# Filter blocks and the shift convolution turned by transposing transfers, with channels on partitions

## The chip, the cores and the metric

The kernel runs on one core of a Trainium2 chip. The metric is the device time of one execution in microseconds (us). The time before is the median of three runs, 225.92 us (225.48 to 226.31).

A core has four computing engines that run beside each other: PE (matrix products; its weight loads are shown as PEld), DVE (elementwise work), ACT (activations, scaled copies), and POOL (small elementwise work). SP only issues transfers. Transfers run on 16 DMA engines. Each engine works through its own list in order and waits on semaphores.

## The reference

```
x = A_q                                   # 2048 x 640, bf16
g = sigmoid(sum(x * gate_w, -1))          # one gate per row

# a: shift convolution, product, long convolution along the sequence, output product
k_shift[s] = sum over t = 0..3 of k[s - t] * shift_k[:, t]
kv = k_shift * v
y  = causal convolution of kv with ssm_k along the sequence, per channel
a  = q * (y + kv * ssm_D)

# b: LayerNorm over channels, then an MLP that mixes the sequence
h = layernorm(x)
u = gelu(h^T w1 + b1)                     # 640 x 1536
b = (u w2 + b2)^T
out = g * a + (1 - g) * b
```

The filter `ssm_k` comes with channels in rows (640 x 2048); q, k and v come with the sequence in rows (2048 x 640).

## The kernel before

The long convolution is cut into P = 4 blocks of n = 512 positions (NB = 4 tiles of 128). Filter block i and input block j are transformed with sine and cosine tables of length 1024. There are four sets of 128 frequencies (fi = 0 and 1 the odd ones, 2 and 3 the even ones), with a cosine and a sine part each. Z for output block m is the sum over j of A_j times W_(m-j), and each Z is transformed back. The products A * W and their sums run on DVE (`pair`); forward and backward transforms run on PE.

The filter: `wnat_load` brings block i with channels on partitions. `w_time` (called for each block ahead of `w_freq`) turns it with 20 matmuls against an identity matrix, and ACT copies four 128x640 results to `wT`. `split` forms sums and differences of the block's halves (`ee`) on DVE. `transform` then makes 48 matmuls per block: two tiles of `ee` per result for even frequencies, four tiles of `wT` for odd ones, the latter with the negated tables `TN`. ssm_D is added to the filter's first position.

The input: `kv_load` brings, for each of the 16 tiles of 128 positions, k with its three predecessors (a row of `k4` holds four rows of k, so k is read four times over), and v. `kv_tile` multiplies `k4` on DVE by `shkb` (shift_k copied to all partitions by eight matmuls), and sums the four taps on PE by matmuls against the identity, or against the flip matrix for the two later tiles of a block, whose v is flipped by PE and ACT as well. ACT copies the sum to `kvb`, DVE multiplies it by v. `a_split` forms sums and differences (`es`), and `a_freq` makes 32 matmuls per block and eight copies on ACT to `A`.

The MLP: `h` has one tile per 128 rows of x; DVE makes the statistics, and POOL the root. The first MLP product takes w1 in six sets of two columns of 128 (`w1_load`), the second takes w2 (`mlp2`).

Nothing of the order is written by hand. All operations are given to a planner (`_Plan`), which books a cost and a latency for each, books a transfer at 0.30 MB per us plus 2 us, and ranks the operations by a priority (the argument `pr`) and by the length of the work that hangs on them. It then places each on its engine in time, which fixes the engine's order. Four results of two PSUM banks each (`_PS`) can be open at once. `_Tracker` places the waits. Every transfer but the later w1 sets and w2 (POOL) is issued from SP. Buffers have fixed places in SBUF; they hold k4 four deep, v five deep, `kvb` and `es` once.

Line numbers in the profile are those of helpers: L290 is every matmul, L676 every DVE tensor_tensor, L718 every ACT operation, L258 every transfer. So work is told apart by its tiles.

Of the kernel before, what the change touches and what calls it, by code (L numbers as in the profile page):

```python
# [17 lines left out]
class _Tracker:  # L18
# [227 lines left out]
    def dma(self, stream, out_ap, in_ap, semname, noncontig=False, accum=False):  # L246
# [5 lines left out]
        if accum:  # L252
            ins = engobj.dma_start(out_ap, in_ap, accum_op=ALU.add)
# [263 lines left out]
def _build(nc, A_q, A_k, A_v, A_shift_k, A_ssm_k, A_ssm_D, B_x, B_w1, B_b1, B_w2, B_b2, gate_w, out):  # L517
# [15 lines left out]
    with ExitStack() as es:  # L533
# [28 lines left out]
        buf("bf", [128, FT + NT], F32, 0, END)  # L562
        buf("brow", [FT + NT, 128], BF16, 0, 30)
# [14 lines left out]
        buf("ident", [128, 128], BF16, 0, END)  # L578
        buf("flip", [128, 128], BF16, 0, END)
        buf("flipn", [128, 128], BF16, 0, END)  # L580
        buf("Dv", [128, D], BF16, 0, 40)
        buf("TFc", [128, 1024], BF16, 0, 48)
        buf("TFs", [128, 1024], BF16, 0, 48)
        buf("TN", [128, 2, 256], BF16, 0, 48)
# [10 lines left out]
        for i in range(P):  # L595
            buf(f"wnat{i}", [128, DC, n], BF16, 0, 16 + 6 * i)
            buf(f"wT{i}", [128, NB, D], BF16, 5 + 5 * i, 24 + 7 * i)
        for i in range(2):
            buf(f"ee{i}", [128, NB, D], BF16, 8, (40, 46)[i])
        for i in range(P):  # L600
            buf(f"W{i}", [128, 9, D], BF16, 14 + 8 * i, END)
        buf("shk1", [1, D, KS], BF16, 0, 20)
        buf("ones", [1, 128], BF16, 0, 20)
        buf("shkb", [128, KS, D], BF16, 5, 84)
        KR = 4
        VR = 5
        for i in range(VR):
            buf(f"v_{i}", [128, D], BF16, 30 + 2 * i, 84)
        KVB = 1
        for i in range(KR):  # L610
            buf(f"k4_{i}", [128, KS, D], BF16, 30 + 2 * i, 84)
        buf("tT", [128, 8, D], BF16, 42, END)
        for i in range(KVB):
            buf(f"kvb{i}", [128, NB, D], BF16, 44, 90)
        for i in range(1):
            buf(f"es{i}", [128, NB, D], BF16, 48, 90)
# [57 lines left out]
        def tt(out_, in0, in1, op, pr, eng="DVE"):  # L674
            c = 0.07 + nel(out_) / 1920.0 if eng == "DVE" else 0.3 + nel(out_) / 500.0
# [46 lines left out]
        def dma(out_ap, in_ap, semname, pr, stream="SP", noncontig=False):  # L722
# [6 lines left out]
            def emit():  # L729
                T.dma(stream, out_ap, in_ap, semname, noncontig=noncontig)  # L730
# [3 lines left out]
        def pe(pslist, mms, pr, after=()):  # L734
# [4 lines left out]
            cost = sum(0.016 + m[2] * 0.000372 for m in mms)  # L739

            def emit():
                full = [(pp[p_.slot][:, c0:c0 + w_], lhsT, rhs, st, sp) for (p_, c0, w_, lhsT, rhs, st, sp) in mms]
                T.mm_part(full)
# [20 lines left out]
        memset(cst[:, 4:5], 2.0 / N2, 0)  # L764
        memset(cst[0:1, 4:5], 0.0, 0)
        memset(cst[:, 5:6], -float(n), 0)
        memset(cst[:, 6:7], -float(N2), 0)
        c_pi, c_hp, c_mh, c_w, c_w0, c_mn, c_mn2 = (cst[:, i:i + 1] for i in range(7))
# [12 lines left out]
        ts(b["ident"][:, :], b["id_i"][:, :], 0.0, None, ALU.is_equal, None, 0.2, eng="POOL")  # L781
# [33 lines left out]
        TN = b["TN"]  # L815
        for nb in range(2):
            c0 = nb * 512 + 256
            ts(TN[:, nb, 0:128], TFs[:, c0:c0 + 128], -1.0, None, ALU.mult, None, 0.5, eng="POOL")
            ts(TN[:, nb, 128:256], TFc[:, c0 + 128:c0 + 256], -1.0, None, ALU.mult, None, 0.5, eng="POOL")
        ts(b["par_i"][:, :], b["ncol_i"][:, 0:1], 1, None, ALU.bitwise_and, None, 0.6, eng="DVE")  # L820
        for nb in range(2):
            ts(TFs[:, nb * 512:nb * 512 + 1], b["par_i"][:, :], -2.0, 1.0, ALU.mult, ALU.add, 0.6, eng="DVE")
# [9 lines left out]

        def to(c, nb, fi):
            if nb < 2:
                return tf((TFc, TFs)[c], nb, fi)
            nb -= 2
            if c == fi:
                return TN[:, nb, fi * 128:fi * 128 + 128]
            return tf((TFs, TFc)[c], nb, fi)
# [66 lines left out]
        dma(b["Dv"][0:1, :], dram(A_ssm_D, 0, [[D, 1], [1, D]]), "Dv", 0.06)  # L906
# [8 lines left out]
        dma(b["brow"][0:FT, :], dram(B_b1, 0, [[128, FT], [1, 128]]), "b", 1.5)  # L915
        dma(b["brow"][FT:FT + NT, :], dram(B_b2, 0, [[128, NT], [1, 128]]), "b", 1.5)
        p_ = _PS()
        pe([p_], [(p_, 0, FT + NT, b["brow"][:, :], b["ident"][0:FT + NT, 0:FT + NT], True, True)], 2)
        act(b["bf"][:, :], (lambda p_: lambda: pp[p_.slot][:, 0:FT + NT])(p_), ACT.Copy, 2, ps=[p_])
        dma(b["shk1"][:, :, :], dram(A_shift_k, 0, [[D * KS, 1], [1, D * KS]]), "shk", 1.6)  # L920
        memset(b["ones"][:, :], 1.0, 2)
        for j in range(KS):
            p_ = _PS()
            pe([p_], halves(p_, [(b["ones"][:, :], b["shk1"][:, :, KS - 1 - j])]), 0.9)
            act(h2(b["shkb"][:, j, :]), two(p_), ACT.Copy, 0.9, ps=[p_])

        def w_time(i):
            wn = b[f"wnat{i}"]
            wT = b[f"wT{i}"]
            for k in range(NB):  # L930
                p_ = _PS()
# [302 lines left out]
```

## Time and profile before

| what | us |
|---|---|
| median of three runs | 225.92 |
| span of the profiled execution, first to last instruction | 222.4 |
| PE busy, 1481 matmuls | 202.8 |
| DVE busy, 253 instructions | 201.8 |
| ACT busy, 221 instructions | 139.9 |
| POOL busy | 41.5 |

The profile has no time of its own execution besides the span; the median lies 3.5 us above that. A group's line reads: engine, operation, tiles written <- read, shapes, count | total busy us, mean ns of one | idle time of the engine just before them, and what ended it. In the chain each line has a start, a length and what ran. In the slices a digit is the busy share in tenths of one fortieth of the span.

### The profile page before, as it was taken

The numbers are of one execution on the slowest core, as the hardware profiler recorded it, in microseconds if no ns is written. First come the engines' busy times: TensorE is split into PE (matmuls) and PEld (weight loads), VectorE is DVE, ScalarE is ACT, GpSimd is POOL, SyncE is SP. The second block draws the span as 40 slices with busy tenths as digits, with TensorE's granted clock in tenths as the row PEclk, the third lists the DMA queues.
The fourth block names the chain that finished last, engine by engine and source line by source line (L and its number), as shares of the span: only waits on it lengthen the run. The fifth ranks groups of instructions, "written<-read, shape, count | busy, mean of one in ns | idle before, by whom it ended". The sixth has DMA issues, their size and how long they took to land.

```text
span 222.4 us, 3751 instructions
## 1 busy us (share of the span) xinstructions
PE 202.8 (91%) x1481; PEld 141.1 (63%) x1481; DVE 201.8 (91%) x253; ACT 139.9 (63%) x221; POOL 41.5 (19%) x79
## 2 busy tenths in 40 slices
PE   0829799999998998999999999999999999999991
PEld 0725547567675774777777777667777777767651
DVE  3379999899988998999999999999999999999771
ACT  4899988997579869683746511799431845432251
POOL 8563330301131010015171010000101101110000
PEclk9988999999999999999999999999999999999997
DMA  6999996139915894899962114302065845286003
GB/s 180 359 325 349 235 298 244 43 109 304 347 41 146 297 391 160 287 295 294 288 181 58 36 16 140 119 3 59 0 202 169 244 116 180 83 253 200 0 3 118
DMA packets 22087, 39.88 MB, mean 179 GB/s; under 512 B 1715, under 2 KB 17205, under 8 KB 22069
## 3 DMA queue, kind: packets, MB, share of 16 engines
q1 hardware_dynamic: 18964, 28.10, 39.8%
q0 software_dynamic: 3104, 11.54, 17.9%
q8 instruction: 12, 0.20, 0.4%
q14 instruction: 7, 0.05, 0.1%
HBM read 36.35 MB, written 2.62 MB: 175 GB/s over the span
## 4 chain that ended last, share of the span: by engine, by line
PE 60%; DVE 22%; ACT 11%; DMA 5%; issue 1%; DVEq 0%; SPq 0%
PE pp L290 60%; DVE Z L676 10%; DVE tT L676 7%; DMA k<-in_A_k_dram 3%; ACT wT L718 2%; ACT W L718 2%; DMA wnat<-in_A_ssm_k_dram 2%; ACT L718 1%; DVE es L676 1%; DVE cg L676 1%; ACT kvb L718 1%; DVE kvb L676 1%; DVE k L676 1%; DVE xg L676 1%; ACT TFs L718 1%
## 5 line engine op out<-in xcount | busy, mean ns | idle before, releaser
L290 PE MATMUL pp<-h,w 128*128 128x320 bf16 x384 | 54.9, 299 | 0.0
L290 PE MATMUL pp<-gT,w 128*128 128x320 bf16 x384 | 53.1, 299 | 0.0
L676 DVE TENSOR_TENSOR tT<-A,W 128x640 bf16<-128x640 bf16 (+4 forms) x44 | 48.0, 1121 | 0.3
L676 DVE TENSOR_TENSOR Z<-Z,tT 128x2560 bf16<-128x2560 bf16 (+3 forms) x35 | 47.1, 1370 | 0.1
L290 PEld LDWEIGHTS pp<-gT,w 128*128 128x128 bf16 x384 | 37.5, 98 | 14.8 <-issue 0.3
L290 PEld LDWEIGHTS pp<-h,w 128*128 128x128 bf16 x384 | 37.5, 98 | 14.6
L258 POOL DMA_DIRECT2D w<-in_B_w_dram x18 | 17.3, 962 | 117.7 <-PE pp L290 117.1
L718 ACT ACTIVATE o<-pp,c,omg 128x640 bf16<-128x640 f32 x16 | 14.2, 884 | 31.4 <-PE pp L290 31.4
L676 DVE TENSOR_TENSOR k<-k,shkb 128x2560 bf16<-128x2560 bf16 x16 | 23.4, 1485 | 0.6 <-DMA k<-in_A_k_dram 0.5
L718 ACT ACTIVATE A<-pp 128x640 bf16<-128x640 f32 x32 | 20.0, 717 | 2.0 <-PE pp L290 2.0
L718 ACT ACTIVATE gT<-pp,bf 128x640 bf16<-128x640 f32 x12 | 9.5, 792 | 18.3 <-PE pp L290 18.2
L290 PE MATMUL pp<-Z,TI 128*128 128x320 bf16 x128 | 18.4, 299 | 1.1 <-ACT kvb L718 1.1
L718 ACT ACTIVATE W<-pp 128x640 bf16<-128x640 f32 x24 | 15.9, 707 | 3.9 <-PE pp L290 3.8
L290 PE MATMUL pp<-ident,wnat 128*128 128x128 bf16 x80 | 8.0, 274 | 10.1 <-DMA wnat<-in_A_ssm_k_dram 5.4
L290 PEld LDWEIGHTS pp<-Z,TI 128*128 128x128 bf16 x128 | 12.4, 98 | 6.4 <-ACT kvb L718 1.4
L718 ACT ACTIVATE kvb<-pp 128x640 bf16<-128x640 f32 x16 | 11.2, 701 | 5.8 <-PE pp L290 5.8
L290 PEld LDWEIGHTS pp<-ident,wnat 128*128 128x128 bf16 x80 | 6.6, 124 | 11.2 <-DMA wnat<-in_A_ssm_k_dram 5.8
L893 DVE BATCH_NORM_STATS2 stats<-xs 128x6 f32<-128x320 bf16 x32 | 13.3, 475 | 0.0
L718 ACT ACTIVATE xg<-xg 128x640 bf16<-128x640 bf16 x16 | 11.6, 734 | 1.7 <-DVE xg L676 1.7
L676 DVE TENSOR_TENSOR Z<-A,W 128x5120 bf16<-128x5120 bf16 x4 | 11.3, 2819 | 0.7 <-ACT A L718 0.7
L290 PE MATMUL pp<-wT,TFc 128*128 128x320 bf16 x48 | 10.1, 300 | 1.7 <-ACT W L718 1.7
L290 PE MATMUL pp<-es,AFs 128*128 128x320 bf16 x64 | 10.1, 300 | 0.8 <-ACT gT L718 0.8
(92 smaller groups left out, 279.2 us busy)
## 6 DMA issues: line engine op xcount, KB each, us to landing
k<-in_A_k_dram SPq DMA_DIRECT2D x15, 640.0 KB, 7.7
w<-in_B_w_dram POOLq DMA_DIRECT2D x8, 768.0 KB, 5.8
w<-in_B_w_dram POOLq DMA_DIRECT2D x10, 512.0 KB, 6.1
wnat<-in_A_ssm_k_dram SPq DMA_DIRECT2D x4, 640.0 KB, 6.5
v<-in_A_v_dram SPq DMA_DIRECT2D x16, 160.0 KB, 7.4
xg<-in_A_q_dram SPq DMA_DIRECT2D x8, 320.0 KB, 7.1
xe<-in_A_q_dram SPq DMA_DIRECT2D x8, 320.0 KB, 3.1
out_dram<-cg SPq DMA_DIRECT2D x8, 320.0 KB, 4.3
```

The source lines that it names most:

```text
L258: ins = engobj.dma_start(out_ap, in_ap)
L290: ins = self.nc.tensor.matmul(ps_ap, lhsT=lhsT, rhs=rhs, start=start, stop=stop)
L676: return vop(eng, c, lambda e: e.tensor_tensor(out_, in0, in1, op), [in0, in1], [out_], pr)
L718: return e.activation(out_, src, func, **kw)
L893: vop("DVE", 0.41, (lambda o_, i_: lambda e: e.bn_stats(o_, i_))(o_, i_), [i_], [o_], pr)
```

## The change

Channels lie on partitions for the filter and for the shift convolution. Transfers that transpose (`dma_start_transpose`, all issued from SP) take the place of turns on PE.

The filter: DVE folds a block while channels are on partitions: the later half plus and minus the earlier half read backwards, from position 256 outwards (`en`); position 0, with D added in block 0, goes into the first column of the difference. One transposing transfer within SBUF turns the fold into `eo`. The transform then takes two tiles for each result, odd or even frequency, 32 matmuls per block, with four more against a row of ones (`onr`, one partition) and four against a column of signs (`nyq`). Results go to a sine or cosine place of W with a sign given by `WMAP`. The tables' first row is set by hand, and `TN` is gone.

The input: per block, k (with 16 rows ahead of it) and v are loaded by one transposing transfer each, 640 KB, into `kT` and `vT`, two deep. The four taps are matmuls of 512 columns against diagonal matrices `dg` (20 blocks of 128x128, made by POOL from the identity and shift_k), the shift being an offset in `kT`. ACT copies three results of 1024, 1024 and 512 columns to `ks`. DVE multiplies the block by `vT` in one instruction, folds it as sum and difference with itself read backwards (into vT's place), and a transposing transfer turns the fold into `es`, now two deep.

ssm_D comes as five more rows of `brow`, turned with the biases by the same matmul, which now comes early. The planner's costs change: tensor_tensor on DVE 0.145 us plus its columns in place of 0.07, a DVE operation behind another 0.02 in place of 0.08, a matmul 0.0235 plus its columns, at least 0.1, in place of 0.016.

```diff
-    SELF = {"PE": 0.0, "ACT": 0.07, "DVE": 0.08, "POOL": 0.1}
+    SELF = {"PE": 0.0, "ACT": 0.07, "DVE": 0.02, "POOL": 0.1}
...
+        if turn:
+            ins = engobj.dma_start_transpose(out_ap, in_ap)
...
+        buf("bf", [128, FT + NT + DC], F32, 0, END)
+        buf("brow", [FT + NT + DC, 128], BF16, 0, 30)
...
+            buf(f"eo{i}", [128, 2, 2, D], BF16, 8, (40, 46)[i])
+            buf(f"en{i}", [128, NB, D], BF16, 5, (30, 36)[i])
...
+        buf("dg", [128, DC, KS, 128], BF16, 5, 84)
+        KR = 2
+        for i in range(KR):
+            buf(f"kT{i}", [128, DC, n + 16], BF16, 30 + 2 * i, 84)
+            buf(f"vT{i}", [128, DC, n], BF16, 30 + 2 * i, 84)
+        buf("ks", [128, DC, n], BF16, 40, 88)
+        for i in range(2):
+            buf(f"es{i}", [128, NB, D], BF16, 48, 90)
...
-            c = 0.07 + nel(out_) / 1920.0 if eng == "DVE" else 0.3 + nel(out_) / 500.0
+            c = 0.145 + nel(out_) / 1920.0 if eng == "DVE" else 0.3 + nel(out_) / 500.0
...
-            cost = sum(0.016 + m[2] * 0.000372 for m in mms)
+            cost = sum(max(0.1, 0.0235 + m[2] * 0.000372) for m in mms)
...
-        TN = b["TN"]
-        for nb in range(2):
-            c0 = nb * 512 + 256
-            ts(TN[:, nb, 0:128], TFs[:, c0:c0 + 128], -1.0, None, ALU.mult, None, 0.5, eng="POOL")
-            ts(TN[:, nb, 128:256], TFc[:, c0 + 128:c0 + 256], -1.0, None, ALU.mult, None, 0.5, eng="POOL")
...
+            ts(b["nyq"][:, nb:nb + 1], b["par_i"][:, :], -2.0, 1.0, ALU.mult, ALU.add, 0.6, eng="DVE")
+            memset(TFs[:, nb * 512:nb * 512 + 1], 0.0, 0.6)
...
+        dma(b["brow"][0:FT, :], dram(B_b1, 0, [[128, FT], [1, 128]]), "b", 0.06)
+        dma(b["brow"][FT:FT + NT, :], dram(B_b2, 0, [[128, NT], [1, 128]]), "b", 0.06)
+        dma(b["brow"][FT + NT:FT + NT + DC, :], dram(A_ssm_D, 0, [[128, DC], [1, 128]]), "b", 0.06)
...
+        dma(b["shd"][:, :, :], dram(A_shift_k, 0, [[KS, 128], [128 * KS, DC], [1, KS]]), "shk", 1.6)
+        copy(b["shf"][:, :, :], b["shd"][:, :, :], 1.7, "POOL")
+        for c in range(DC):
+            for j in range(KS):
+                ts(b["dg"][:, c, j, :], ident, b["shf"][:, c, j:j + 1], None, ALU.mult, None, 1.8, eng="POOL")
+
+        def w_turn(i):
             wn = b[f"wnat{i}"]
-            wT = b[f"wT{i}"]
-            for k in range(NB):
-                p_ = _PS()
-                mms = [(p_, c * 128, 128, wn[:, c, k * 128:(k + 1) * 128], b["ident"][:, :], True, True)
-                       for c in range(DC)]
-                pe([p_], mms, 1.0 + 0.1 * i)
-                act(wT[:, k, :], flat(p_), ACT.Copy, 0.3, ps=[p_])
+            en = b[f"en{i % 2}"]
+            eo = b[f"eo{i % 2}"]
+            fw = wn[:, :, 256:512].rearrange("p c (k u) -> p k c u", k=2)
+            bw = bass.AP(tensor=wn, offset=256, ap=[[DC * n, 128], [-128, 2], [n, DC], [-1, 128]])
+            for e, op in ((0, ALU.add), (1, ALU.subtract)):
+                tt(en[:, 2 * e:2 * e + 2, :].rearrange("p k (c u) -> p k c u", c=DC), fw, bw, op, 1.0 + 0.1 * i)
+            x0 = en[:, 2, :].rearrange("p (c u) -> p c u", c=DC)[:, :, 0:1]
...
+            dma(eo[:, :, :, :].rearrange("p e k (c d) -> p (e k c) d", c=DC),
+                en[:, :, :].rearrange("p k d -> p (k d)"), f"eo{i % 2}", 0.5, turn=True)
...
         def w_freq(i, pr):
...
+                    pairs = [(tf((TFc, TFs)[c], nb, fi), eo[:, c, nb, :]) for nb in range(2)]
+                    if c == 0 and fi >= 2:
+                        sg = 3 - fi
+                        pairs.append((b["onr"][:, sg * 128:(sg + 1) * 128], eo[0:1, 1, 0, :]))
+                    if c == 1 and fi == 3:
+                        pairs = pairs[:1] + [(b["nyq"][:, nb:nb + 1], eo[:, 0, nb, :]) for nb in range(2)] + pairs[1:]
...
+        def kv_load(i, pr):
+            nm = f"kT{i % KR}"
+            if i == 0:
+                memset(b[nm][:, :, 0:16], 0.0, 3.3)
+                dma(b[nm][:, :, 16:16 + n], dram(A_k, 0, [[D, n], [1, D]]), nm, pr, turn=True)
             else:
+                dma(b[nm][:, :, :], dram(A_k, (i * n - 16) * D, [[D, n + 16], [1, D]]), nm, pr, turn=True)
+            nm = f"vT{i % KR}"
+            dma(b[nm][:, :, :], dram(A_v, i * n * D, [[D, n], [1, D]]), nm, pr, turn=True)
+
+        def kv_block(i, pr):
+            kT, vT = b[f"kT{i % KR}"], b[f"vT{i % KR}"]
+            ks = b["ks"]
+            en = vT[:, :, :].rearrange("p c t -> p (c t)").rearrange("p (k d) -> p k d", k=NB)
+            for c0, cn in ((0, 2), (2, 2), (4, 1)):
                 p_ = _PS()
+                mms = [(p_, (c - c0) * n, n, b["dg"][:, c, j, :], kT[:, c, 16 - j:16 - j + n], j == 0, j == KS - 1)
+                       for c in range(c0, c0 + cn) for j in range(KS)]
+                pe([p_], mms, 1.1)
+                act(ks[:, c0:c0 + cn, :], (lambda p_, cn: lambda: pp[p_.slot][:, 0:cn * n].rearrange(
+                    "p (c t) -> p c t", c=cn))(p_, cn), ACT.Copy, 1, ps=[p_])
+            tt(ks[:, :, :], ks[:, :, :], vT[:, :, :], ALU.mult, pr - 2)
+            fw = ks[:, :, 0:256].rearrange("p c (k u) -> p k c u", k=2)
+            bw = bass.AP(tensor=ks, offset=n - 1, ap=[[DC * n, 128], [-128, 2], [n, DC], [-1, 128]])
+            for e, op in ((0, ALU.add), (1, ALU.subtract)):
+                tt(en[:, 2 * e:2 * e + 2, :].rearrange("p k (c u) -> p k c u", c=DC), fw, bw, op, pr - 2)
+            dma(b[f"es{i % 2}"][:, :, :].rearrange("p k (c d) -> p (k c) d", c=DC),
+                en[:, :, :].rearrange("p k d -> p (k d)"), f"es{i % 2}", 3.0, turn=True)
```

More of the change, by code (lines that the diff above doesn't have):

```diff
@@ L919, in _build @@
[L919 to L922, printed above, removed]
-            p_ = _PS()
-            pe([p_], halves(p_, [(b["ones"][:, :], b["shk1"][:, :, KS - 1 - j])]), 0.9)
-            act(h2(b["shkb"][:, j, :]), two(p_), ACT.Copy, 0.9, ps=[p_])
-        def w_time(i):
-            wn = b[f"wnat{i}"]
-            wT = b[f"wT{i}"]
-            for k in range(NB):
-                p_ = _PS()
-                mms = [(p_, c * 128, 128, wn[:, c, k * 128:(k + 1) * 128], b["ident"][:, :], True, True)
-                       for c in range(DC)]
-                pe([p_], mms, 1.0 + 0.1 * i)
-                act(wT[:, k, :], flat(p_), ACT.Copy, 0.3, ps=[p_])
-            if i == 0:
-                tt(wT[0:1, 0, :], wT[0:1, 0, :], b["Dv"][0:1, :], ALU.add, 1.1)
+        pe([p_], [(p_, 0, FT + NT + DC, b["brow"][:, :], ident[0:FT + NT + DC, 0:FT + NT + DC], True, True)], 0.06)
@@ L1054, in kv_two @@
         def kv_two(i):
[L1055 to L1060 removed]
+            kv_load(i, 8.0 + 3 * i)
+            kv_block(i, 11.0 + 2 * i)
         def z_split(m_):
```

126 lines of the change are left out of this document (35 added, 91 removed).

## The prediction

> **What bounds the kernel now.** I read the page's busy shares and slices first, then the stretches of 5 and 10 us, the chain, and the groups by shape.
>
> ```profile
> PE 202.8 (91%) x1481; PEld 141.1 (63%) x1481; DVE 201.8 (91%) x253; ACT 139.9 (63%) x221; POOL 41.5 (19%) x79
> ...
> PE   0829799999998998999999999999999999999991
> ...
> DVE  3379999899988998999999999999999999999771
> ...
> DMA  6999996139915894899962114302065845286003
> ...
> DMA packets 22087, 39.88 MB, mean 179 GB/s; under 512 B 1715, under 2 KB 17205, under 8 KB 22069
> ```
>
> PE and DVE are both nearly full from about 17 us to the end; the DMA engines are full only to about 35 us.
>
> ```profile
> 10.00:15.00 5.00, 1.28 (x15) 0.77 (x15) 2.93 (x8) 4.97 (x8) 1.82 (x3) 1.00 1.09 323
> ...
> 25.00:30.00 5.00, 3.49 (x27) 2.30 (x25) 5.00 (x19) 4.83 (x9) 2.11 (x4) 1.00 1.07 241
> ...
> 110.00:120.00 10.00, 10.00 (x76) 7.22 (x74) 9.90 (x8) 5.27 (x10) 5.07 (x5) 1.00 0.48 136
> ```
>
> Columns: PE, PEld, DVE, ACT, POOL, then clock, DMA share, GB/s. Early, ACT is full and PE waits for it; later PE has no gap.
>
> ```profile
> 28.05 15.48 PE pp L290 x101
> ...
> 54.83 1.49 DVE k L676
> ...
> 148.40 63.92 PE pp L290 x468
> ```
>
> The chain runs mostly on PE. Its last long piece gives the price of a 320-column matmul: 63.92/468 = 0.1366 us.
>
> ```profile
> L676 DVE TENSOR_TENSOR k<-k,shkb 128x2560 bf16<-128x2560 bf16 x16 | 23.4, 1485 | 0.6 <-DMA k<-in_A_k_dram 0.5
> ...
> L718 ACT ACTIVATE kvb<-pp 128x640 bf16<-128x640 f32 x16 | 11.2, 701 | 5.8 <-PE pp L290 5.8
> ...
> L676 DVE TENSOR_TENSOR ee<-wT 128x1280 bf16<-128x1280 bf16 x8 | 6.4, 820 | 3.0 <-ACT wT L718 2.0 <-PE pp L290 0.9
> ```
>
> The sum is made against the span, 222.4 us; the median of the three times, 225.92, lies 3.5 above it, which I add at the end.
>
> **PE.** Gone: 80 turns of wnat (the first 40 took 3.78 us, so 7.6); 8 broadcasts of shift_k (2.4); 128 tap matmuls and 16 flips of v (144 x 0.1366 = 19.7); of the filter transform's 192 matmuls 32 (4.4), since two foldings replace four blocks for the odd frequencies, with 4 extra halves for the row of ones and 4 for the Nyquist column per block. New: 20 matmuls of 512 columns per block, 80 in all. No row has 512 columns: by columns 0.1366 x 512/320 = 0.2186, so 17.5 (at 0.1366 each it would be 10.9; at two of 320, 21.9). I take 17.5, as 320 columns already run column by column with the weight loads (98 ns) hidden. The turns lie before 18 us, where PE idles anyway; in the full part PE saves 2.4 + 19.7 + 4.4 - 17.5 = 9.0 us.
>
> Checked from the bottom: 1216 matmuls x 0.1366 + 17.5 = 183.6 us must run after the first transform. Now it is 1393 x 0.1366 + 2.4 = 192.7 from 17.9 us; with about 5 us of tail this leaves 6.8 us of gaps in 222.4.
>
> **When PE can start.** wnat lands at 5.4 us. Two folds (0.82 each) and the D add follow; the add waits for a row of bf, now loaded and turned early (three small loads, at 0.4 to 0.9 us of SP each, ahead of xs). Then one transfer turns 640 KB within SBUF. The sine tables, which waited on ACT behind eight wT evictions, come about 5 us earlier. The first transform starts at about 9 us plus a turn, so 16 to 18 us, as now. Buffers en and eo are two deep, so blocks 2 and 3 wait for transforms 0 and 1: two more turns are exposed before 45 us, where PE has the first MLP set (64 matmuls, 8.7 us) and the first taps to fill with, if those are ready.
>
> **One turning transfer.** The trace has none. By bytes: 58.2% of 222.4 us for 39.88 MB is 308 GB/s, so 0.655 MB takes 2.1 us of all engines. By pieces: 22,087 packets in 129.4 us x 16 engines is 94 ns each; 2,560 pieces of 256 bytes (128 rows turned) would take 15 us. Between them: from 110 to 120 us, when w1's 512-byte rows move, 136 GB/s at share 0.48 is 283 GB/s, 29 ns a row; pieces of 256 bytes at that price make 4.6 us. I take t = 4.6, the row nearest in piece size, and keep 2.1 and 15. The quiet first wnat needed 4.65 to land, 2.5 above its bytes, so a turn lands after about 7.1. A gain below 2.1 I exclude: no stretch moved over 400 GB/s.
>
> The Trainium skill, "DMA: Bandwidth & Descriptors", section "Latency and other measured facts", gives 261 GB/s for a measured kernel's transposing transfers; by it, as an estimate, a turn is 2.5 us, the first start 2 us earlier, and the total some 213.
>
> There are 16 turns (k, v, filter and kv folds, four each): 74 us of DMA at t. Gone are 13.1 MB (k four times over, and v), 43 us. So DMA goes from 129 to about 160 us of busy share: not a bound over the whole, but early it is full. SP issues 35 k and v loads fewer and 16 turns more. A plain 640 KB issue takes SP 0.4 to 0.6 us; a turn's own issue may be that or as long as its transfer, and behind the filter turns on SP stand xs, w1 and kT loads. The first of these turns adds the longest wait: SP stands until both folds and the D add are done, and the add, in DVE's order, until bf has come through SP, PE and ACT; behind it on SP are xs and w1, behind the add on DVE the tables' index work. Each microsecond SP stands makes xs as late; DVE has 2 us free in 10 to 15 us, and h is needed tile by tile until 42 us, so 2 us are covered, and beyond that they cost one for one.
>
> **DVE.** Gone: 23.4 (k times shkb), 7.6 (16 products with v), 6.4 and 6.2 (splits), 0.5. New: 4 products of 2560 (5.9), 16 folds of 1280 with one operand read backwards, and 4 tiny copies (0.6). A fold is 0.82 by the ee row if the backward operand costs nothing; if DVE falls to one element a cycle, as the cast of 640 from PSUM does (0.82 for 640), it is 1.49. So 19.6 to 30.3 new against 44.1: DVE saves 24 to 14 us, and ends below PE either way. I take 0.82; the other end moves nothing unless PE waits.
>
> **ACT.** Gone: 16 wT (9.7), 4 shkb (2.5), 8 v (5.4), 16 kvb (11.2). New per block: 1024, 1024 and 512 columns. From 188 ns for 28 and 704 for 640 columns a column is 0.84 ns: 1.03 + 1.03 + 0.60, four times 10.6. Net -18 us, of which 12 in the phase where ACT is full; this takes away most of the 6.8 us that PE and its loads waited for W evictions there.
>
> **POOL.** 20 diagonal blocks at 0.57 (the flipn row; TN took 0.52 to 0.87) are 11.4 us, and ten small memsets 2; gone are TN 2.7 and the k memset 1.7. POOL is idle four fifths after 20 us. Each diagonal ahead of an rstd delays one h by 0.6 us, covered by the statistics; it would cost its length only if h were what PE waits for. shift_k arrives in 640 runs of 8 bytes: at 29 to 94 ns each, 1.2 to 3.8 us of DMA, needed only for the taps at about 40 us. The planner's new constants cost nothing themselves; they reorder.
>
> **Sum.** Start 18, work 183.6, gaps 5 (6.8 now, less 5 of ACT waits, plus 3 for turns not hidden), tail 5: 211.6, plus 3.5, is 215 us. Least: start 15, gaps 1: 208 with t = 4.6; with faster taps, 206.
>
> **Rivals.** A. Turns are slow (slower than before). A0 needs 6.8 MB of wnat, xs and w1 (22 us), six turns (four filters, kT0, vT0), then taps 4.4, eviction 0.6, product 1.5, folds 1.6, one turn with 2.5, and about 5 from es to the first pair (58.3 to 63.3 now): 38 + 7t. Behind A0 DVE has 107.5 us of pair work, 18 of epilogue, some 6 of the rest, and 5 of tail: end = A0 + 137. At t = 4.6, A0 comes at 70 and DVE ends at 207, below PE. It decides from A0 = 85, that is t = 6.7. At t = 9: 101 + 137 + 3.5 = 241; at t = 15, 283. For it: pieces cost more than bytes in this trace (94 ns per packet). Against: the 512-byte rows still ran at 283 GB/s. Chance 0.26.
> The Trainium skill, "VectorE: DVE Perf Modes", section "The three transpose paths", gives 1309 ns for a 128x128 turn by DMA; were the 20 blocks of a transfer run one after another, t would be 26 and this rival would hold, and no row here shows which.
>
> B. Turns land later than the planner books. It books 0.655/0.30 + 2.0 = 4.2 us; at 7.1, PE, whose order is fixed, stands up to 2.9 us at each of eight turns, 23 us in all. With half of it hidden: 215 + 12 = 227. For it: before, PE already stood at wnat (5.4 us); against: other work lies between. 225 to 229, half of it within 0.5%. Chance 0.12.
>
> C. Backward operands at half rate, or the odd start of the filter's backward half: inside the forecast, 215 to 219.
>
> **Numbers.** Forecast 0.62 (206 to 222), A 0.26, B 0.12. Faster by over 0.5% (about what measurement can tell from no change here): 0.62; within: 0.06; slower: 0.06 + 0.26 = 0.32. The range 206 to 240 reaches half into A. Faster alone: 206 to 222.
>
> **What would show it.** PE's taps at about 0.22 us and PE busy near 187; DVE near 177 (188 if the backward read halves the rate); turns landing near 7 us, Z's first product near 70. Wrong if turns land beyond 9 us, if SP's turn issues last microseconds and xs lands late, or if PE stands before transforms of es.

## The result and the profile after

The changed kernel takes 232.43 us (median of four, 230.45 to 234.76) against 225.82 for the kernel before. The ratio is 1.026, with an interval of 1.021 to 1.031: slower by 2.6%, where 215 us was forecast. The comparisons leave disturbed runs out, so a ratio here can differ a little from the quotient of two medians. The profiled execution was the longest of the four, 234.76 us; its span, from the first to the last instruction, is 232.9.

The page of the changed kernel, its busy shares, three rows of the slices, and the packets:

```profile
PE 193.5 (83%) x1297; PEld 121.8 (52%) x1297; DVE 179.3 (77%) x228; ACT 122.4 (53%) x189; POOL 50.8 (22%) x104
...
PE   0003999705999999999997999999998999999992
...
PEclk9999999965999999999999999999999999999999
DMA  6999999999876955199963033110175554476011
...
DMA packets 59859, 37.29 MB, mean 160 GB/s; under 512 B 43587, under 2 KB 57027, under 8 KB 59843
```

The work of DVE and ACT fell as forecast, by 22.5 and 17.5 us; that of PE fell by 9.3, where some 16 were forecast (187 us busy). PE now starts late and has a hole in slices 8 and 9, and the DMA engines are full for 58 us where they were full for 35. There are 41,900 more packets under 512 bytes.

The stretches around the hole (columns: PE, PEld, DVE, ACT, POOL busy, granted clock, DMA share, GB/s):

```profile
40.00:45.00 5.00, 5.00 (x36) 3.23 (x33) 3.59 (x5) 3.34 (x6) 0.00 (x0) 1.00 1.05 195
45.00:50.00 5.00, 0.01 (x1) 0.00 (x0) 1.61 (x2) 1.17 (x2) 1.43 (x3) 0.84 1.18 224
50.00:55.00 5.00, 0.18 (x1) 0.10 (x1) 0.00 (x0) 0.00 (x0) 0.00 (x0) 0.50 1.12 205
55.00:60.00 5.00, 5.00 (x21) 1.57 (x21) 0.00 (x0) 1.59 (x3) 0.00 (x0) 0.63 1.02 208
```

PE stands almost 10 us, then gets 21 matmuls through in 5 us where the stretch before the hole has 36: the granted clock fell to 0.50 during the stand. One of PE's waits (us in total, times, longest) and two pieces of the chain name what PE waited for, the filter's turns (`eo`):

```profile
PE pp L290 <- DMA eo<-en: 23.4, 2, 13.6
```

```profile
44.21 10.47 DMA eo<-en
54.81 24.35 PE pp L290 x136
```

SP's own timeline (start, length of the issue, what was issued) shows how the third turn came so late:

```profile
11.39 1.91 SPq L258 DMA_DIRECT2D xs<-in_A_q_dram  x3
13.35 9.07 SPq L253 DMA_TRANSPOSE eo<-en  x2
22.46 0.59 SPq L258 DMA_DIRECT2D xs<-in_A_q_dram  x1
23.09 3.87 SPq L253 DMA_TRANSPOSE kT<-in_A_k_dram  x1
27.00 0.58 SPq L258 DMA_DIRECT2D w<-in_B_w_dram  x1
27.63 3.30 SPq L253 DMA_TRANSPOSE vT<-in_A_v_dram  x1
30.98 0.58 SPq L258 DMA_DIRECT2D w<-in_B_w_dram  x1
31.61 3.28 SPq L253 DMA_TRANSPOSE kT<-in_A_k_dram  x1
34.93 6.30 SPq L253 DMA_TRANSPOSE vT<-in_A_v_dram  x1
...
44.21 10.46 SPq L253 DMA_TRANSPOSE eo<-en  x2
```

Both folds were ready by 9.1 us (DVE's last piece of them is the line below), but eight xs loads and two of w stood ahead of the turn on SP: it was issued at 13.35 and landed at 21.4.

```profile
8.90 0.17 DVE L687 COPY en<-wnat 128x5 bf16<-128x5 bf16 x1
```

Then the turns of k and v held SP for 3.3 to 6.3 us each, where the planner books 0.5, and the third filter turn waited behind them.

The account against the span, by the forecast's own four terms, in us: start 21.4 (forecast 18), PE busy after that 193.3 (183.6), tail 4.4 from the last matmul (5), so gaps are 232.9 - 21.4 - 193.3 - 4.4 = 13.8 (5). Work and gaps, some 9 us each, carry the miss, the late start 3.4.

### The profile page after: what moved, and what is told of

It reads as the page before. It is cut to its first block, busy times and chain, and to the rows that moved or that the text cites. A ratio compares the mean times of both kernels' runs of the same rounds, so it can differ in the third digit from the quotient of the medians.

```text
span 232.9 us, 3304 instructions
## 1 busy us (share of the span) xinstructions
PE 193.5 (83%) x1297; PEld 121.8 (52%) x1297; DVE 179.3 (77%) x228; ACT 122.4 (53%) x189; POOL 50.8 (22%) x104
## 3 DMA queue, kind: packets, MB, share of 16 engines
q0 software_dynamic: 3104, 11.54, 17.5%
## 4 chain that ended last, share of the span: by engine, by line
PE 62%; DMA 16%; SPq 10%; DVE 5%; issue 3%; ACT 2%; POOL 1%; POOLq 0%; DVEq 0%; ACTq 0%
PE pp L290 62%; DMA w<-in_B_w_dram 8%; SPq L253 7%; DMA eo<-en 4%; DVE stats L886 4%; DMA xs<-in_A_q_dram 3%; SPq L258 3%; DMA xg<-in_A_q_dram 1%; ACT W L714 1%; DVE mv L888 0%; ACT o L714 0%; POOL w L258 0%; DVE pb L1142 0%; DVE cg L672 0%; ACT cg L714 0%
## 5 line engine op out<-in xcount | busy, mean ns | idle before, releaser
L290 PE MATMUL pp<-eo,TFs 128*128 128x320 bf16 x64 | 13.3, 319 | 23.4 <-DMA eo<-en 23.4
L714 ACT ACTIVATE o<-pp,c,omg 128x640 bf16<-128x640 f32 x16 | 14.2, 885 | 30.5 <-PE pp L290 30.5
L672 DVE TENSOR_TENSOR W<-W,W 128x2560 bf16<-128x2560 bf16 x6 | 9.0, 1492 | 23.1 <-ACT W L714 23.0
L290 PEld LDWEIGHTS pp<-eo,TFs 128*128 128x128 bf16 x64 | 5.6, 99 | 29.5 <-issue 27.0
L714 ACT ACTIVATE W<-pp,cst 128x640 bf16<-128x640 f32 x8 | 6.4, 794 | 25.0 <-PE pp L290 25.0
L290 PE MATMUL pp<-kT,dg 128*128 128x512 bf16 x80 | 18.1, 379 | 0.0
L714 ACT ACTIVATE xg<-xg 128x640 bf16<-128x640 bf16 x16 | 11.6, 731 | 9.2 <-DVE xg L672 9.2
L290 PE MATMUL pp<-eo,TFc 128*128 128x320 bf16 x64 | 13.5, 315 | 0.2 <-ACT W L714 0.2
L679 POOL TENSOR_SCALAR dg<-idp,shf 128x128 bf16<-128x128 bf16 x20 | 13.0, 676 | 0.1
```

The source lines that it names most:

```text
L290: ins = self.nc.tensor.matmul(ps_ap, lhsT=lhsT, rhs=rhs, start=start, stop=stop)
L672: return vop(eng, c, lambda e: e.tensor_tensor(out_, in0, in1, op), [in0, in1], [out_], pr)
L679: return e.tensor_scalar(out_, in0, s1, None, op0=op0)
L714: return e.activation(out_, src, func, **kw)
```

## The experiments

The experiments set these theories against each other: **S**, a turn holds SP by itself, and SP's fixed order does the rest (O, later: order and depth of buffers decide). **D**, small pieces fill the DMA engines. **M**, or N, the narrow matmuls (a weight of 1x128 or 128x1) are dear. **C**, formed on the way: a turn and a weight load of POOL's software queue slow each other.

### What the turns cost: plain transfers in their place

```diff
-dma(b[nm][:, :, :], dram(A_v, i * n * D, [[D, n], [1, D]]), nm, pr, turn=True)
+dma(b[nm][:, :, :], dram(A_v, i * n * D, [[DC * n, 128], [n, DC], [1, n]]), nm, pr)
```

(and so for all 16; the output is then not the reference's, but PE, DVE and ACT do the same work in the same order)

> All sixteen turning transfers become plain transfers of the same bytes between the same buffers, so k, v and both folds are not turned and the output is not the reference's; instructions of all engines and their order stay. Theory S with D (turns cost what plain transfers do not, on SP and on the DMA engines): SP issues them in 0.4 to 1 us each, the first transform starts at 15 to 18 us, the stand of 9.8 us falls under 2, time 215 to 221. Theory M alone: PE's surplus lies in the narrow matmuls, the time stays above 228.

Measured: 223.21 us, ratio 0.987 (0.980 to 0.993), no hole. So the change's other work is a gain, and the transposing transfers lose it. The gain is smaller than was expected, and PE still started at 20.8 us: the late start is not the turns' doing, but that of what stands ahead of them. The second run keeps plain transfers but cuts them into 2,560 pieces of 256 bytes (all but the first of k, whose pieces have 1 KB):

```diff
+dma(bass.AP(tensor=b[nm], offset=0, ap=[[DC * n, 128], [128, 20], [1, 128]]), dram(A_v, ...), nm, pr)
```

> The 16 turns become plain transfers again, but cut into the turns' pieces: 2,560 pieces of 256 bytes each (264 for k with its margin) instead of whole rows of 1,280 bytes. The bytes, the order of all work and the arithmetic stay; what the transfers bring is not turned, so the output is not the reference's. Theory S (a transposing transfer holds SP by its own nature, since the transposed pieces are made out while SP stands): plain pieces cost SP no more than plain rows, issues 0.4 to 2.6 us as with whole rows, time 222 to 225. Theory D (the pieces themselves fill the engines and their queues, and SP stands because the queue is full): SP's issues last 2.5 to 6 us as for turns, PE stands at 45 to 55 us, time 229 to 234. Between (some 3 us of SP, 226 to 228) both have a part.

Measured: ratio 0.994 (0.989 to 0.999), times from 223 to 232 us. The issue of es, in a quiet stretch, in the tile's rows (ns: shortest, median, longest); first the plain pieces, then the turns of the changed kernel:

```profile
L258 SPq DMA_DIRECT2D es<-vT x4: 606/659/676, 50.9 to 102.9; - x4
```

```profile
L253 SPq DMA_TRANSPOSE es<-vT x4: 2475/2584/4490, 58.6 to 110.6; - x4
```

The same pieces cost SP 0.66 us plain and 2.58 transposing: S holds for SP's time. When the engines are full a plain issue of pieces can last as long (5.2 us, the longest of eo), so D has a part. On the DMA engines the two are alike: a piece takes 18 ns at the median in both traces, and in their best 2 us the pieces moved at 272 GB/s plain and at 288 turning. In time, what the pieces cost is too little to tell (0.987 and 0.994, with intervals that overlap); transposing them costs 3%.

### Which half loses

> The kernel before with one half of the change: k and v come by transposing transfers, taps by diagonals, folds of kv and four turns of es; the filter keeps its 80 turns on PE, its wT evictions, its splits and its four-block odd transform. Planner constants as before. The forecast's items for this half: PE -2.4 -19.7 +17.5, DVE -23.4 -7.6 -6.4 +5.9 +6.6, ACT -19.1 +10.6. Theory S and D alike (the loss sits in the filter's turns, at the start and at 45 to 55 us): no stand of PE at 45 to 55 us, start at about 18 us, 217 to 223. Rival K (the turns of k and v cost as much, issued at 2.5 to 6 us each on SP): 226 or more.

> The changed kernel with the other half alone: the filter is folded on VectorE and turned by four transposing transfers, with the narrow matmuls for the row of ones and the Nyquist column; k and v are loaded four rows to a partition and multiplied on VectorE as before. Theory M (narrow matmuls cost 5 us, late start 3 us, against a gain of 4.4 us of PE and 16 to 18 us of ACT's early time): 224 to 230, near the kernel before. If the loss of the whole change sits in the filter's turns whatever else is on SP: 229 to 234, PE starts at 20 us or later and stands in the middle. If the stand needs the turns of k and v on the same queue: PE starts at 18 to 20 us, no stand beyond 3 us.

The half with k and v alone: 225.5 us (221.0 to 230.5), too far apart to tell it from the kernel before; in its profiled execution PE waited once 7.0 us for a weight load, in a stretch of 89 GB/s at a full DMA share. The filter half alone: ratio 1.049 (1.040 to 1.058), worse than the whole change. Its turns on SP, amid k and v loads of the old kind:

```profile
12.86 12.94 SPq L253 DMA_TRANSPOSE eo<-en  x2
41.95 13.56 SPq L253 DMA_TRANSPOSE eo<-en  x2
```

Four turns hold SP for 26.5 us (19.5 in the whole change), with no other turns beside them. So the length of an issue depends on the other loads as well; that it follows how full the engines are is the likely reading, not shown by itself.

### The place of the turns

Moving the k and v turns of block 1 behind the filter's third and fourth:

```diff
+                    after=turns[2:] if i == 1 else ())
```

> Block 1's k and v turns are planned behind the filter's third and fourth turn, all else as in the changed kernel. Theory S (a turn holds SP 2.5 to 6 us and the planner books 0.5; the two turns of block 1, 9.6 us, stand on SP ahead of the filter's third): PE's stand of 9.8 us shrinks to 1 to 3 us, the clock does not fall to a half behind it, time 220 to 225. Theory D (the DMA engines are full to 58 us, in whatever order): the stand moves to block 1's taps or to MLP sets, time 229 to 233.

Measured: ratio 1.042 (1.035 to 1.049); my expectation under S missed. The third turn was issued at 35.7 us and the hole at 45 to 55 us closed (8.67 of 10 us busy), but PE then stood at 65 to 75 us (6.01 of 10; the trace names ACT's copies of A, 6.6 us). Shifting turns shifts the hole, which speaks for D beside S.

Giving en and eo four buffers instead of two:

```diff
-            buf(f"eo{i}", [128, 2, 2, D], BF16, 8, (40, 46)[i])
+            buf(f"eo{i}", [128, 2, 2, D], BF16, 8, (40, 46, 46, 46)[i])
```

> en and eo get a buffer for each filter block, so no turn waits for an earlier transform. Theory S: the filter's third and fourth turn go ahead of block 1's k and v on SP, the stand before them falls from 9.8 us to under 3, time 220 to 225. Theory D: the third turn is earlier, but x and w1 come later by as much, time 228 to 232.

Measured: ratio 1.012 (1.007 to 1.016), where D put it. No hole at 45 to 55 us (9.88 of 10 busy), but the planner put more loads ahead of the first turn, and PE started at 24.7 us.

Narrow matmuls made full tiles padded with zeros:

```diff
-        buf("onr", [1, 256], BF16, 0, 40)
+        buf("onr", [128, 256], BF16, 0, 40)
```

> The row of ones and the Nyquist column become full 128x128 tiles padded with zeros; same sums, same order, all else as in the changed kernel (ratio to before 1.026, about 232). Theory M (matmuls with one row or one column cost about 0.2 us more than a full one when they alternate with full ones; 32 of them, about 5 us): TFc and TFs groups run at 0.137 us a matmul without the 0.26 us weight waits, PE busy falls by 4 to 5 us, the time by 2 to 5, as the first half of it only lengthens the wait for the third filter turn: 227 to 230. Theory S (the order on SP and the length of the turns): the stand of PE before the third turn stays, at 10 to 12 us.

Measured: ratio 1.017 (1.011 to 1.023), some 2 us less than the change; PE busy 190.8, 2.7 less. What is saved ahead of the hole only lengthens the hole (10.7 us). The price of the narrow matmuls is plain in PE's timeline; the changed kernel, then full tiles, both at full rate:

```profile
28.77 0.45 PE L290 MATMUL pp<-eo,TFc 128*128 128x320 bf16 x2
29.15 0.30 PE L290 MATMUL pp<-eo,onr 1*128 1x320 bf16 x1
29.39 0.45 PE L290 MATMUL pp<-eo,TFc 128*128 128x320 bf16 x2
```

```profile
26.05 0.43 PE L290 MATMUL pp<-eo,TFc 128*128 128x320 bf16 x2
26.32 0.30 PE L290 MATMUL pp<-eo,onr 128*128 128x320 bf16 x1
26.45 0.43 PE L290 MATMUL pp<-eo,TFc 128*128 128x320 bf16 x2
```

A group of three starts every 0.62 us with the narrow weight, every 0.40 with the full one; a group of four with nyq every 0.74 against 0.55. 16 x 0.22 + 8 x 0.19 = 5.0 us in all by these distances; PE's busy time fell by about half of that in this run, in which the clock was halved for longer.

Then all of it: four deep, full tiles, the filter's turns due first, and the planner told what SP's rows show.

```diff
-            return plan.add(stream, 1.2 if stream == "POOL" else 0.5, emit, [in_ap], [out_ap], pr, dma=max(tot, 20000) / 1e6)
+            return plan.add(stream, 1.2 if stream == "POOL" else (3.0 if turn else 0.9), emit, [in_ap], [out_ap], pr,
+                            dma=max(tot, 20000) / 1e6 * (1.5 if turn else 1.0))
...
-                en[:, :, :].rearrange("p k d -> p (k d)"), f"eo{i % 2}", 0.5, turn=True)
+                en[:, :, :].rearrange("p k d -> p (k d)"), f"eo{i}", -20, turn=True)
```

> The changed kernel with en and eo four deep, the narrow matmuls made full 128x128 tiles padded with zeros, and the planner told what the profile shows of SP: a plain load 0.9 us, a turn 3.0 us and half more transfer time; the filter's four turns are due first and stand on SP after three of the xs loads. Theory: the start comes when the second fold is turned, 16 to 19 us, no stand in the middle, and 3 us less of PE by the full tiles: 222 to 227, the early gain of ACT showing. Rival X (the loads of xs and w1 that now stand behind 12 us of turns come late and VectorE's statistics with them): PE waits for h at 25 to 40 us, 227 to 232.

Measured: 217.81 us, ratio 0.967 (0.962 to 0.971): faster than before, and by more than expected. Its relatives, first without the full tiles, then with two buffers, then with shift_k loaded early:

> As turns_first_full_tiles (217.8 us), but with the narrow matmuls of the change: the row of ones as a 1x128 weight, the Nyquist column as a 128x1 weight. Tells the part of the full tiles from the part of the order. Theory O (order and depth decide; narrow matmuls cost 32 times 0.15 to 0.2 us at full rate and keep TensorE at half rate longer after its first start): 3 to 6 us more, 221 to 224, still faster than the kernel before. Rival N (the narrow matmuls are the loss of the whole change, the order is worth little): 226 or more.

> As turns_first_full_tiles, but with en and eo two deep as in the change: the first two turns can go first, the third and fourth must wait until the transform of blocks 0 and 1 has read its buffer. Theory O with depth (the stand in the middle comes from turns that wait for a buffer and then for the queue): TensorE starts at 16 to 18 us but stands again for 4 to 10 us before block 2, 221 to 228. If only the place and the planner's costs matter, the third turn being planned at its true length: no stand beyond 3 us, 217 to 221.

> As turns_first_full_tiles, but the load of shift_k and its cast are due early, so that it stands on SP ahead of the xs loads and the diagonals are made before 30 us instead of 31 to 49 us. There TensorE had 5.0, 4.4, 3.7 and 3.8 us busy in the four stretches from 30 to 50 us and waited for the diagonals and for evictions of W. If the late diagonals are what is left: those 3 us are filled, 213 to 216.5. If they only hide a wait behind them (loads of xs and h, W on ACT): 217 to 219.

Narrow: ratio 1.016 (1.008 to 1.024). Two deep: 217.4 to 234.5 us, too far apart to compare; in its trace the third turn made PE wait 1.4 us only, weight loads 6.8. Taps early: ratio 1.005 (0.998 to 1.012), times from 224 to 233 us. So one small edit after another cost up to 5%. Each edit also makes the planner order the work anew, on PE, DVE and ACT too, so a difference between two such kernels holds that as well. Narrow came out where N put it, but its trace gives another reason (below); taps early, expected at 219 us or less, missed by 5 us and more. The planner's constants by themselves:

> The kernel before with nothing but the changed planner constants (VectorE's extra per operation 0.02 for 0.08 us, a tensor_tensor's base 0.145 for 0.07 us, a matmul's cost at least 0.1 us with base 0.0235 for 0.016 us). Tells whether the other order that they give costs by itself. My theory books it at nothing: 224 to 227. If it is 229 or more, part of the loss is the planner's and not the turns'.

Measured: ratio 1.005 (1.001 to 1.009), a microsecond.

### The collision with POOL's weight loads

What differed between these relatives was in the transfers. Narrow stood 7.7 us for a weight load at 111 to 119 us, taps early 8.4 us for the first kT, which landed 19.7 us after its issue. DMA rows of two windows of 4 us: taps early at 38 to 42 us, then the changed kernel at 54 to 58.

```profile
DMA packets 651, 0.33 MB, mean 84 GB/s; under 512 B 607, under 2 KB 607, under 8 KB 651
...
q1 hardware_dynamic: 601, 0.15, 89.0%
q0 software_dynamic: 50, 0.18, 34.7%
```

```profile
DMA packets 3717, 0.94 MB, mean 236 GB/s; under 512 B 3717, under 2 KB 3717, under 8 KB 3717
...
q1 hardware_dynamic: 3717, 0.94, 115.8%
```

q1 is SP's queue, q0 POOL's; the last column is the time that their packets took, as a share of 16 engines' time (packets overlap, so it can exceed 100%). In the first window, with POOL's queue at work, a piece of a turn takes 0.89 x 16 x 4 / 601 = 95 ns on average; in the second, without it, 1.158 x 16 x 4 / 3717 = 20 ns. Plain pieces of the same size do not suffer from POOL's queue: at 31 to 35 us of plain_in_256_byte_pieces they take 1.107 x 16 x 4 / 3401 = 21 ns.

```profile
q1 hardware_dynamic: 3401, 0.89, 110.7%
q0 software_dynamic: 62, 0.25, 16.5%
```

So the weight loads were moved to the turns' own queue (in three kernels), or to ACT's:

```diff
-                        f"{nm}_{t0}" if s_ < 1 else f"{nm}_p", pr + 0.35 * (8 * hf + t0), stream="SP" if s_ < 1 else "POOL")
+                        f"{nm}_{t0}" if s_ < 1 else f"{nm}_p", pr + 0.35 * (8 * hf + t0), stream="SP" if s_ < 1 else "SP")
...
-                stream="POOL")
+                stream="SP")
```

> The changed kernel, with the 18 weight loads of 512 KB that POOL issues (software queue) issued by SP instead, on the hardware queue that carries the turns. Theory C (a turn and a weight load of the software queue that are under way together slow each other: in turns_first_taps_early 30 to 46 us and turns_first_narrow 106 to 118 us the hardware queue moved 600 to 1,130 pieces in 4 us, with the software queue idle 3,100 to 3,700): in the changed kernel this shows only at 50 to 54 and 76 to 78 us, so the stand at 45 to 55 us shrinks by 2 or 3 us and the time is 227 to 231. Theory S (SP's own order and issue time): SP now holds 18 issues of 0.9 us more, no gain or a loss: 231 to 236.

> As turns_first_taps_early (229.0 us, two stands of TensorE before kT, of 8.4 and 3 us, in stretches where the engines were full at 62 to 134 GB/s), with the weight loads on SP's hardware queue. Theory C: no stretch under 140 GB/s at a full share, kT lands in 6 to 9 us instead of 11.6 (median) and 19.7 (longest), 213 to 219. If a turn from the device's memory is slow by itself, or SP's time is what counts: 226 to 232.

> As turns_first_narrow (228.3 us, of which 7.7 us in one wait for a weight load at 111 to 119 us and the half-rate clock after it), with the weight loads on SP's hardware queue. Theory C: that wait goes, and what is left beside turns_first_full_tiles (217.8) is the price of the narrow matmuls, 3 to 6 us: 219 to 224. If the wait stays: 226 to 230.

> As turns_first_taps_early, with the weight loads issued by ACT on its own hardware queue: a second queue beside that of the turns, but not the software queue. If it is the software queue that collides: as on SP, 213 to 219. If any second queue does: 225 to 232, with stretches under 140 GB/s at a full share.

> Control: the kernel before, which has no turns, with its 18 weight loads on SP's hardware queue. Theory C (a collision of turns with the software queue): without turns nothing to gain, 225 to 228. If the software queue costs time by itself, here too: 220 to 223, and the gain of weights_on_sp says nothing of the turns.

| kernel | ratio, weights on POOL | ratio, weights elsewhere |
|---|---|---|
| the change | 1.026 (1.021 to 1.031) | SP 1.002 (0.997 to 1.006) |
| turns first, narrow | 1.016 (1.008 to 1.024) | SP 0.973 (0.964 to 0.981) |
| turns first, taps early | 1.005 (0.998 to 1.012) | SP 0.983 (0.976 to 0.990), ACT 0.975 (0.969 to 0.982) |
| turns first, full tiles | 0.967 (0.962 to 0.971) | SP 0.960 (0.955 to 0.965) |
| the kernel before | 1 | SP 1.002 (0.997 to 1.007) |

Three of the kernels with turns gain 2 to 4%, the kernel without turns nothing. The fourth, turns first with full tiles (its run on SP stands under "Everything mended"), gains 0.7%, with intervals that overlap, and its trace on POOL's queue has no stretch of 4 us under 140 GB/s at a full share. So the harm goes with turns and the software queue together; on a second hardware queue, ACT's, the same loads did no such harm. In turns first, narrow and in taps early the long waits for w and kT are gone from PE's list. The change had none of these; there the hole at 45 to 55 us closed: the last turn ahead of the third filter turn held SP for 3.0 us in place of 6.3, that filter turn went out at 41.1 us in place of 44.2, and PE also came to it later, for another reason (below).

Three things these runs do not separate. On SP and ACT the weights came in pieces of 512 bytes, on POOL's queue in packets of 3.6 KB, so it may be the size of the packets. POOL loses its 18 issues (busy 50.8 to 34.5 us in the changed kernel). And the planner orders the work anew. Nor is the software queue the only way to a slow stretch: under 110 GB/s over 4 us at a full share is seen in four traces with turns and the software queue, but once without it as well (taps_early_weights_on_sp, 94 GB/s at 88.5 to 92.5 us). Taps early still came out above 219 us on either queue, 1 to 3 us above what was expected; on SP, PE stood once more, 7.2 us for ACT. Open stays why the collision strikes only sometimes: in turns_first_full_tiles a turn of es and a weight load were under way together from 102 to 114 us at 203 to 326 GB/s.

Two of these traces suggest that narrow matmuls can cost more than their groups. PE after its first start, weights_on_sp, then full_tiles (columns as above):

```profile
25.00:30.00 5.00, 5.00 (x17) 1.14 (x16) 3.97 (x10) 1.51 (x3) 4.67 (x9) 1.00 1.15 238
30.00:35.00 5.00, 5.00 (x17) 1.19 (x16) 5.00 (x20) 1.69 (x3) 4.24 (x13) 1.00 1.03 280
```

```profile
25.00:30.00 5.00, 5.00 (x39) 3.60 (x38) 3.68 (x9) 4.31 (x7) 4.67 (x11) 1.00 1.10 244
```

PE starts at 21.5 and 21.7 us. With full tiles it reaches its rate 2.8 us later, with narrow ones it ran at half rate for 16 us, though the clock column says 1.00 throughout; the doubled distances are seen in the timeline alone. In the changed kernel this took 3.2 us after the first start and 3.8 after the hole; over all kernels 3 to 19 us with narrow matmuls (19 in narrow_weights_on_sp), 2.8 to 6 with full tiles. Narrow matmuls do not decide it alone: the change and the two plain runs have the same order of work on PE, and there it was 3.2, 4.2 (plain rows) and 16 us (plain pieces). That the narrow ones stretch it, and why only at times, was not tried by itself.

### Everything mended

> The version that takes in every repair: filter buffers four deep, the filter's turns first, full tiles for the narrow matmuls, weight loads on SP's queue. turns_first_full_tiles (217.8 us) had 18 us of gaps and warming after its start. Theory C: as fast as that or a little faster, 213 to 218. If SP, with 18 more issues, holds the es turns up: 218 to 223.

Measured: 216.36 us (215.90 to 217.03), ratio 0.960 (0.955 to 0.965), the fastest of all. Its busy row and PE's longest waits (the first two lie ahead of the small matmul of the biases and ahead of the first transform):

```profile
PE 189.4 (88%) x1292; PEld 124.1 (58%) x1297; DVE 179.0 (84%) x228; ACT 122.7 (57%) x189; POOL 34.1 (16%) x89
```

```profile
PE pp L290 <- POOL nyq L690: 7.7, 1, 7.7
PE pp L290 <- DVE stats L889: 7.4, 1, 7.4
PE pp L290 <- ACT W L714: 2.8, 8, 0.9
PE pp L290 <- DVE Z L672: 1.3, 1, 1.3
```

After the start no wait for a transfer is left. The way there from the change: weights on SP, 226.97 us; filter turns first and four deep, with the planner's new costs, 219.99; full tiles, 216.36. By ratio 2.4, 2.9 and 1.3 per cent of the time before.

## Why the prediction was wrong

**Work: right for DVE, ACT and POOL, not for PE.** DVE was forecast at 177 and came to 179.3, ACT saved 17.5 (18), POOL rose by 9.3 (9). PE was forecast at 187 and came to 193.5. Groups of the changed kernel by shape:

```profile
L290 PE MATMUL pp<-kT,dg 128*128 128x512 bf16 x80 | 18.1, 379 | 0.0
L672 DVE TENSOR_TENSOR en<-wnat 128x1280 bf16<-128x1280 bf16 x8 | 6.3, 834 | 1.5 <-DMA wnat<-in_A_ssm_k_dram 1.5
L672 DVE TENSOR_TENSOR vT<-ks 128x1280 bf16<-128x1280 bf16 x8 | 6.2, 821 | 0.1
L290 PEld LDWEIGHTS pp<-eo,onr 1*128 1x128 bf16 x16 | 1.5, 91 | 4.9 <-issue 4.9
```

The 80 taps took 18.1 us (17.5 worked out from columns). Folds took 0.83 and 0.82 us, the lower end: backward operands, from position 256 (filter) or 511 (kv), cost nothing, and rival C is out.

**The 183.6 us of work failed in the narrow matmuls.** It priced all 32 like full ones, at 0.1366 each. By the distances in the timeline they cost 5 us more, and the weight loader stands idle before them (4.9 us for onr). PE's half-rate stretches have no term of their own: 3.2 + 3.8 us, of which half, 3.5, is lost. With 0.6 from the taps that is 9.1 of the 9.7 us. The split is an estimate: the kernel before was busy for 195.0 us after 17.9 us too, where the forecast's price gives 192.7, so some 2 us of busy time above the price were there already, among its 6.8 us of gaps; and with full tiles everywhere PE is still busy for 189.4 us.

The Trainium skill, "TensorE: Matmul & The Clock Gate", section "What's actually happening", says that an idle array runs at half clock and warms in about 3.4 us of sustained work. The traces with full tiles (2.8 and 6 us) and of the change agree roughly; the 16 and 19 us with narrow tiles are longer than the page leads one to expect.

**Start: 18 forecast, 21.4 measured.** The step "the first transform starts at about 9 us plus a turn" left out what stands ahead of the turn on SP. The folds were done at 9.1 as worked out; the issue came 4.3 us later. Plain transfers in the same place left the start at 20.8 us; with the turn due first PE started at 15.3 us (turns_first_weights_on_sp).

**Gaps: 5 forecast, 13.8 measured; this is the step that failed most.** "Plus 3 for turns not hidden" priced a turn by its landing, and let SP go on after half a microsecond, though the text named the other end ("a turn's own issue may be that or as long as its transfer"). That end was the true one: 2.5 us in quiet, 3 to 6 when the engines are full. With two buffers the third turn waits for block 0's transform, which ended at 30.7 us. It went out 13.5 us after that. In plain_for_turns and in order_k1_later the transform ended at 30.5 and 32.8 us, and the third transfer went out 2.9 us after it:

```profile
33.38 3.16 SPq L258 DMA_DIRECT2D eo<-en  x2
```

```profile
35.72 8.19 SPq L253 DMA_TRANSPOSE eo<-en  x2
```

So the two turns of block 1 that stand ahead of it on SP, 9.6 us, and SP's fixed order made it some 10 us late. The size t itself was priced too high: from 54 to 56 us, where only turns ran, they moved 288 GB/s, and from 54 to 58 us 236: 2.3 to 2.8 us for 0.655 MB (4.6 taken); es landed after 4.4 us at the median (7.1).
The Trainium skill's 261 GB/s ("DMA: Bandwidth & Descriptors", section "Latency and other measured facts") would make 2.5 us of it; the trace agrees. The Trainium skill's 1309 ns for one 128x128 turn ("VectorE: DVE Perf Modes", section "The three transpose paths") does not add up over 20 blocks: 26 us were never seen, the longest landing of a turn in any trace being 22.9 us (turns_first_two_deep) and the shortest 4.1.

**The rivals.** What came is B, turns later than the planner books, with PE standing in its fixed order; its 225 to 229 was too low, since the stand also halves the clock and since it took SP's time and POOL's queue for free. The measured 232 us lies inside the 206 to 240 of the prediction, but only by luck: that range reached up for A, and A is not what happened. A's price, t above 6.7, was met only by single turns in slow stretches: at 95 ns a piece 2,560 pieces are 15 us of all engines, the upper end named. A's sign, the first product of Z late, did appear:

```profile
L672 DVE TENSOR_TENSOR Z<-A,W x4: 2812/2817/2819, 86.5 to 146.7; 128x5120 bf16<-128x5120 bf16 x4
```

It started at 86.5 us in the changed kernel, where near 70 was forecast, and at 69.7 with everything mended. By A's own sum DVE would then end at 86.5 + 137 = 223.5 us, before the 232.9 measured, so it is PE's line that sets the end. Of the signs of being wrong, turns that land beyond 9 us (10.5 at the longest) and SP's issues of microseconds with a late xs (the last went out at 22.5 us) came; PE never stood before a transform of es. So the gain forecast, 215 us, was there to be had (216.4); the change as it was made did not have it.

## What to carry to other kernels

When a transfer of a new kind takes the place of computing, price the time of the queue that issues it, what stands ahead of it there, and what the planner believes of both, before pricing its bytes. Keep the software queue's traffic apart from transposing transfers, and look at the GB/s of a stretch beside its DMA share: full engines at 80 GB/s are a collision, not a load. PE that stands for 10 us pays again in its clock. Test a transfer's cost with a plain transfer in its place: it leaves the order of all other work as it is.

## What the hardware showed that was not expected

- The issue of one 640 KB turn holds SP for 2.5 us when all is quiet and for 3 to 6 in the changed kernel when the DMA engines are full (11.6 at the longest, a vT of taps early); the same pieces untransposed take 0.66, whole rows 0.5.
- A piece of 256 bytes in a turn takes 18 to 20 ns of an engine, as a plain piece does; over 4 us it took 95 ns on average while POOL's software queue moved weights of 3.6 KB a packet, and kT then landed after 19.7 us. A plain piece beside the same queue took 21 ns. The Trainium skill, "Advanced Engine Details and Errata", section "X-Bar Transpose (TRN2)", calls transposing transfers as fast as regular ones; that holds here against plain transfers in the same pieces (288 and 272 GB/s in the best 2 us), not against plain whole rows in their place (up to 395 in a slice).
- Between full tiles, a 1x128 weight costs 0.22 us a group and a 128x1 pair 0.19, and PE's half-rate stretch after the first start was 3 to 19 us long with them, 2.8 to 6 with full tiles.
- Operands read backwards ran at the full rate of DVE (0.82 us for 1280 elements).
